# Low halves of g made by accumulating Pool transfers, row squares kept beside the x2 rows, and weight totals asked for three places later

## The chip, the core and the metric

The kernel runs on one core of one Trainium2 chip. The metric is the time of one execution in microseconds (us) on that core, taken as the median of several runs. The engines are named as in the profile: PE (TensorE), DVE (VectorE), ACT (ScalarE), POOL (GpSimd) and SP (SyncE, which here only issues transfers). Each engine works through its own instructions in order, and waits on semaphores for the others.

## The reference

Attention, a gated linear layer, and a routed layer with eight experts follow each other on 4608 tokens:

```python
scores = scale * np.matmul(q, k.transpose(0, 1, 3, 2))      # 8 x 8 heads, 576 x 576, block causal mask
...
attn = attn / (np.sum(attn, axis=-1, keepdims=True) + 1e-09)
return np.matmul(attn, v).astype(np.float32)
...
a = x @ w1                                                  # 512 -> 1024
b = x @ w2
h = a * b @ w3
return (h @ w_out).astype(np.float32)
...
logits = x @ w_gate                                         # 8 experts
order = np.argsort(-flat)
for idx in order:                                           # greedy: best pair first, 576 tokens per expert
    tok, e = (int(idx) // E, int(idx) % E)
    if assigned[tok] >= 0 or counts[e] >= cap:
        continue
    assigned[tok] = e
...
h = np.maximum(x[mask] @ w1[e], 0.0)                        # 512 -> 1024 -> 512
out[mask] = h @ w2[e]
```

## The kernel before

Products must be nearly exact, so every operand is split into a high half (rounded) and a low half (what the rounding lost), and each product is three matmuls: high by high, high by low, low by high.

The program has three stages. In the first (0 to about 838 us in the profile) attention runs head pair by head pair, and the products `a * b` of the gated layer (called g) are written to a DRAM tensor `gd`. `w3 @ w_out` has been multiplied out into one matrix of 1024 x 512, kept as `W34[0]` (high) and `W34[1]` (low), written by `load_w34`. At the end of this stage the logits of the router are formed.

In the second stage (about 838 to 1137 us) two things share PE. The **route** is a serial search: 7 phases of 9 levels, and in each level PE and DVE hand small results to each other. DVE makes `M` (L789), PE counts with it (L806), DVE makes `mk` (L821), PE sums it (L827), DVE makes `fl` (L830), PE sums it (L832), DVE makes `dl` (L834), and the next `M` follows. Between these small matmuls the **stream** is laid: `x2 = g @ W34`, 36 tiles of 128 tokens with 24 matmuls each (L965). `fill(n)` puts the next n stream matmuls into PE's program at that place, some 10 in each level. PE, Pool and ACT keep the order in which this stage is written (`manual_schedule`); the other engines' order, and all engines' order outside the stage, is set at build time by a scheduler that simulates the program.

A stream tile j needs its g split: `prep_g(j)` loads 128 tokens of g into `g32` (two buffers), ACT rounds them to the high half `gh` (L980), and DVE subtracts to get the low half `gl` (L982, two instructions). It is called two tiles ahead. When a tile is done, `x2_out` copies it from PSUM into `row` (ACT, L988) and SP stores it in the DRAM tensor `xr`. Weights of the first experts (`ew0`) are converted in the same stage, on ACT (L1038) and DVE (L1039).

In the third stage (from about 1137 us) the tokens of each expert are gathered from `xr` by Pool (`xg`, L1090, four buffers). ACT squares the row and adds it up (L1094), DVE turns the sum into a power of two (`pow2`), ACT scales to the high half (L1096), DVE makes the low half (L1097), and SP transposes (`xT`, L1098). PE then does `layer1` (L1121) and `layer2` (L1138) of each expert, while ACT and DVE prepare the next experts' weights in `expert_w`: load, eight squares (`red`, L1024), a matmul with ones that adds the squares over the partitions (`fin`, the **total**, L1029), and eight conversions (`conv`, L1038 and L1039). The list of these operations is interleaved with the list of matmul units in equal shares. The staging buffer of each weight (`esa`, `esb`) exists once, so a load waits until the last conversion before it is done.

Of the kernel before, what the change touches and what calls it, by code (L numbers as in the profile page):

```python
# [7 lines left out]
F32 = mybir.dt.float32  # L8
F32R = mybir.dt.float32r
F16 = mybir.dt.float16  # L10
BF16 = mybir.dt.bfloat16
I32 = mybir.dt.int32
AF = mybir.ActivationFunctionType
ALU = mybir.AluOpType
# [45 lines left out]
def moe_kernel(ctx, tc, q, k, v, moe_w1, moe_w2, moe_w3, moe_w_out, w_gate, ew1, ew2, out):  # L60
# [882 lines left out]

    xr = dram.tile([NTOK, DM], F32, name="xr")
    wl = pb.enter_context(tc.tile_pool(name="wl", bufs=1, reuse_waits="tile"))
# [4 lines left out]
    def load_w34():  # L950
        for f in range(0, 8, 2):
            t = gp.tile([P, 8, P], F32, name="g32").rearrange("p (f a) b -> p f (a b)", f=2)
            nc.sync.dma_start(t, w34d[f:f + 2].rearrange("f p d -> p f d"))
            nc.scalar.activation(W34[0][:, f:f + 2], t, AF.Copy)
            nc.gpsimd.tensor_tensor(out=W34[1][:, f:f + 2], in0=t, in1=W34[0][:, f:f + 2].bitcast(F32), op=ALU.subtract)

# [19 lines left out]
    def prep_g(j):  # L976
        g = gp.tile([P, 8, P], F32, name="g32")
        nc.sync.dma_start(g, gd[:, :, j * P:(j + 1) * P].rearrange("f p t -> p f t"))
        gh = [gp.tile([P, 8, P], F32R, name=f"g{z}") for z in "hl"]
        nc.scalar.activation(gh[0], g, AF.Copy)  # L980
        for f in range(0, 8, 4):
            nc.vector.tensor_tensor(out=gh[1][:, f:f + 4], in0=g[:, f:f + 4], in1=gh[0][:, f:f + 4].bitcast(F32),  # L982
                                    op=ALU.subtract)
        gt[j] = gh

    def x2_out(j, p):
        row = gp.tile([P, DM], F32, name="row", bufs=3)
        nc.scalar.activation(row, p, AF.Copy)  # L988
        nc.sync.dma_start(xr[j * P:(j + 1) * P], row)
# [93 lines left out]
    def gather(p):  # L1083
        def block(h):
            if h == 0:
                xT2[p] = ce.tile([P, 8, NG * P], F16, name="xT2")
                scs[p] = ce.tile([P, NG], F32, name="sc")
            xg = ce.tile([P, DM], F32, name="xg", bufs=4)
            c = p * NG + h
            nc.gpsimd.indirect_dma_start(out=xg, out_offset=None, in_=xr,  # L1090
                                         in_offset=bass.IndirectOffsetOnAxis(ap=idx[:, c:c + 1], axis=0))
            x16 = ce.tile([P, 2, DM], F16, name="x16", bufs=4)
            sq = ce.tile([P, 1], F32, name="sq2", bufs=4)
            nc.scalar.activation(x16[:, 1], xg, AF.Square, accum_out=sq)  # L1094
            s, i = pow2(ce, sq, "xsc", TBX, bufs=4)
            nc.scalar.activation(x16[:, 0], xg, AF.Copy, scale=s)  # L1096
            nc.vector.scalar_tensor_tensor(x16[:, 1], xg, s, x16[:, 0], op0=ALU.mult, op1=ALU.subtract)  # L1097
            nc.sync.dma_start_transpose(out=xT2[p][:, :, h * P:h * P + P], in_=x16.rearrange("p z d -> p (z d)"))  # L1098
            nc.vector.tensor_copy(scs[p][:, h:h + 1], i)

        return [lambda h=h: block(h) for h in range(NG)]
# [47 lines left out]
    def weights(e, part):  # L1149
        if (e, part) == (1, 1):  # L1150
            return owed_w
        return expert_w(e, part, 512, False) if 2 <= e < E else []

    for f in gather(0):
        f()
    for p_ in range(E // 2):
# [7 lines left out]
        interleave([lambda k_=k_: layer2(p_, k_) for k_ in range(4)],  # L1164
                   (expert_w(1, 1, 512, False) if e == 0 else []) + weights(e + 2, 0))
        interleave(list(layer1(e + 1, halves)), more[4:])
# [38 lines left out]
```

## Time and profile before

| | us |
|---|---|
| three runs | 1576.71, 1581.57, 1591.8 |
| median of the three | 1581.57 |
| the profiled execution's own time | 1578.55 |
| its span in the profile | 1576.7 |
| PE busy in the span | 1370.9 (87%) |
| DVE busy | 1031.7 (65%) |
| ACT busy | 909.0 (58%) |
| POOL busy | 93.4 (6%) |

The profile is of one execution. Its own time lies 1.9 us above its span, and 3.0 us below the median of the runs. PE is busiest, but the share is a mean over three stages with different limits, so the stages have to be read one by one.

### The profile page before, as it was taken

Reading aid. Unit: us, or ns where it says so; the run is one execution under the profiler, and the core shown is the slowest. Engines: PE = TensorE matmul, PEld = TensorE weight load, DVE = VectorE, ACT = ScalarE, POOL = GpSimd, SP = SyncE. Lnnn points to the kernel's source line nnn. Section 1 sums busy time; section 2 is a strip of 40 time slices with the busy share of each in tenths; the row PEclk is TensorE's granted clock in tenths of the full one; section 3 lists DMA queues with packets and bytes.
Section 4 is the critical chain, followed back from the end, with each engine's and each line's share of the span. In section 5 each row is a group of like instructions: output and inputs, shape, how many; then the busy total and the mean of one; then the engine's idle time right before and its main releaser. Section 6 shows DMA issues by size and latency. Waiting matters only on the chain. (4 is left out here: it accounts for less than half of the span.)

```text
span 1576.7 us, 32324 instructions
## 1 busy us (share of the span) xinstructions
PE 1370.9 (87%) x12622; PEld 932.3 (59%) x12622; DVE 1031.7 (65%) x3058; ACT 909.0 (58%) x2173; POOL 93.4 (6%) x101
## 2 busy tenths in 40 slices
PE   3457887999898999999999988899669979799897
PEld 2335665666666666666666665666466546466663
DVE  8889998868978887864215778878656543532510
ACT  8879886778868786654221223342167864855611
POOL 0000000000000000100200000000043300110001
PEclk9668999999999999999999999999789989899999
DMA  7767796887868785479945324333297653622200
GB/s 252 179 157 186 192 224 155 177 150 179 214 129 200 161 201 99 92 188 240 307 135 186 101 81 152 97 130 97 89 183 221 157 176 94 187 74 76 72 27 34
DMA packets 379657, 238.51 MB, mean 151 GB/s; under 512 B 261232, under 2 KB 344688, under 8 KB 378480
## 3 DMA queue, kind: packets, MB, share of 16 engines
q1 hardware_dynamic: 372064, 215.46, 53.8%
q0 software_dynamic: 5760, 18.88, 3.7%
q8 instruction: 99, 1.62, 0.4%
q10 hardware_dynamic: 1680, 2.11, 0.4%
q14 instruction: 54, 0.44, 0.1%
HBM read 132.60 MB, written 39.85 MB: 109 GB/s over the span
## 5 line engine op out<-in xcount | busy, mean ns | idle before, releaser
L325 PE MATMUL ab<-xT,w1h 128*128 128x288 f16 x1536 | 218.1, 291 | 14.1 <-ACT a_sb L330 10.7
L325 PE MATMUL ab<-xT,w2h 128*128 128x288 f16 x1536 | 219.5, 292 | 3.3 <-DVE g L335 2.1
L1121 PE MATMUL pe<-xT,ewa 128*128 128x288 f16 (+2 forms) x1728 | 200.7, 281 | 18.8 <-DMA xT<-x 13.6
L1121 PEld LDWEIGHTS <-ewa 128*128 128x128 f16 x1728 | 161.6, 102 | 56.9 <-issue 19.6
L1138 PE MATMUL pe<-ewb,h 128*128 128x512 f16 (+1 forms) x960 | 189.1, 379 | 0.0
L325 PEld LDWEIGHTS <-w1h 128*128 128x128 f16 x1536 | 145.3, 100 | 64.8 <-issue 24.1
L245 ACT ACTIVATE E<-S,nb,cc 128x128 f32<-128x128 f32 (+4 forms) x288 | 181.5, 639 | 2.8 <-DVE P L256 1.0
L325 PEld LDWEIGHTS <-w2h 128*128 128x128 f16 x1536 | 147.3, 100 | 57.0 <-issue 15.2
L256 DVE SCALAR_TENSOR_TENSOR P<-E,rr,P 128x512 f16<-128x512 f32 (+4 forms) x288 | 156.0, 573 | 10.7 <-ACT P L255 10.1
L980 ACT ACTIVATE gh<-g 128x1024 fp32r<-128x1024 f32 x36 | 38.1, 1059 | 204.2 <-issue 181.7
L1138 PEld LDWEIGHTS <-h 128*128 128x128 f16 (+1 forms) x960 | 85.3, 101 | 99.1 <-issue 2.6
L300 PE MATMUL PV<-PT,v 128*64 128x128 f16 (+1 forms) x2880 | 101.5, 223 | 48.0 <-DMA PT<-P 41.1
L1124 DVE SCALAR_TENSOR_TENSOR h<-pe,h 128x288 f16<-128x288 f32 (+2 forms) x144 | 58.8, 420 | 115.5 <-ACT h L1123 115.2
L300 PEld LDWEIGHTS <-v 128*64 128x64 f16 x2880 | 84.0, 117 | 73.3 <-issue 35.6
L965 PE MATMUL px<-W34l,gh 128*128 128x512 f32 x288 | 123.0, 427 | 0.0
L965 PE MATMUL px<-W34h,gh 128*128 128x512 f32 x288 | 122.4, 425 | 0.0
L335 DVE SCALAR_TENSOR_TENSOR g<-ab,vr,a_sb 128x288 f32<-128x288 f32 x124 | 63.5, 512 | 89.9 <-PE ab L325 74.1
L965 PE MATMUL px<-W34h,gl 128*128 128x512 f32 x288 | 122.2, 424 | 0.0
L255 ACT ACTIVATE P<-E,rr 128x128 f16<-128x128 f32 (+3 forms) x176 | 97.4, 604 | 23.9 <-DVE rr L249 15.6
L237 DVE TENSOR_REDUCE nb<-S 128x2 f32<-128x1024 f32 (+3 forms) x128 | 101.5, 813 | 3.6 <-PE S L228 3.5
L1123 ACT ACTIVATE h<-pe 128x288 f16<-128x288 f32 (+2 forms) x144 | 52.3, 378 | 85.4 <-PE pe L1121 85.4
L330 ACT ACTIVATE a_sb<-ab 128x288 f32<-128x288 f32 x128 | 52.2, 408 | 83.3 <-PE ab L325 79.0
(283 smaller groups left out, 2220.4 us busy)
## 6 DMA issues: line engine op xcount, KB each, us to landing
g<-gd SPq DMA_DIRECT2D x36, 512.0 KB, 3.8
gd<-g SPq DMA_DIRECT2D x62, 288.0 KB, 3.0
g<-gd SPq DMA_DIRECT2D x15, 1152.0 KB, 7.1
raw<-in_moe_w_dram SPq DMA_DIRECT2D x32, 512.0 KB, 4.5
esa<-in_moe_w_dram SPq DMA_DIRECT2D x8, 2048.0 KB, 8.7
esb<-in_moe_w_dram SPq DMA_DIRECT2D x8, 2048.0 KB, 9.5
v<-in_v_dram SPq DMA_DIRECT2D x8, 1280.0 KB, 6.2
xr<-row SPq DMA_DIRECT2D x36, 256.0 KB, 2.0
```

The lines of the kernel that those rows point to most:

```text
L237: nc.vector.tensor_reduce(nb[:, 0, k_:k_ + 2], ps[:, :, o:o + N], axis=AX.X, op=ALU.max)
L245: nc.scalar.activation(ef[:, a], pf_[:, a], AF.Exp, bias=nb[:, 1, x:x + 1], scale=c[:, 0:1], accum_out=sums[:, x:x + 1])
L255: nc.scalar.activation(hi, ef[:, at[x]], AF.Copy, scale=r[:, 1, x:x + 1])
L256: nc.vector.scalar_tensor_tensor(lo, ef[:, at[x]], r[:, 1, x:x + 1], hi, op0=ALU.mult, op1=ALU.subtract)
L300: nc.tensor.matmul(ps[hh * 64:hh * 64 + 64, c0:c0 + w], vt[:, zv, hh, j, :], s, start=z == 0 and j == 0, stop=z == 2 and j == nj - 1)
L325: nc.tensor.matmul(p[:, :288], w[:, zw, cc, :], x[:, zx, cc, c0:c0 + 288], start=first, stop=cc == 3 and zw == 1)
L335: nc.vector.scalar_tensor_tensor(g, ps["w2"][:, :288], iv[b][:, f:f + 1], a, op0=ALU.mult, op1=ALU.mult)
L965: nc.tensor.matmul(p, gh[a][:, f], W34[b][:, f], start=f == 0 and a + b == 0, stop=f == 7 and a == 1)
L1121: nc.tensor.matmul(p[:, :n], w1[:, a, cc, f * P:(f + 1) * P], t[:, 4 * b + cc, x], start=cc == 0 and a + b == 0, stop=cc == 3 and a == 1)
L1123: nc.scalar.activation(h[:, 0, f, x], p[:, :n], AF.Relu)
L1124: nc.vector.scalar_tensor_tensor(h[:, 1, f, x], p[:, :n], 0.0, h[:, 0, f, x], op0=ALU.max, op1=ALU.subtract)
L1138: nc.tensor.matmul(p[r0:r1], h[:, a, f, k_ * P + r0:k_ * P + r1], EW[e, "b"][0][:, b, f], start=f == 0 and a + b == 0, stop=f == 7 and a == 1)
```

## The change

Three edits are made at once.

1. **Low halves.** The low half of g is no longer a DVE subtraction. ACT writes the negated high half into the low half's tile (a copy with scale -1), and the high half as before; a Pool transfer with `accum_op=ALU.add` then adds g to the negated half in SBUF, which leaves g minus its high half. The four low halves of `W34`, which Pool subtracted, are made in the same way. `gh` and `gl` get three buffers in place of two.
2. **Row squares.** `x2_out` squares the finished tile straight from PSUM on ACT and adds it up into a 513th column of `row`. `xr` and `xg` get rows of 513 numbers, and the gather block no longer squares what it has gathered. `row` gets two buffers in place of three.
3. **Totals.** `expert_w` is asked for with `early=True` for the later experts, which puts three empty operations between the last square and the total.

```diff
-    xr = dram.tile([NTOK, DM], F32, name="xr")
+    xr = dram.tile([NTOK, DM + 1], F32, name="xr")
...
+            nc.scalar.activation(W34[1][:, f:f + 2], t, AF.Copy, scale=-1.0)
             nc.scalar.activation(W34[0][:, f:f + 2], t, AF.Copy)
-            nc.gpsimd.tensor_tensor(out=W34[1][:, f:f + 2], in0=t, in1=W34[0][:, f:f + 2].bitcast(F32), op=ALU.subtract)
+            nc.gpsimd.dma_start(W34[1][:, f:f + 2].bitcast(F32), t, accum_op=ALU.add)
...
-        gh = [gp.tile([P, 8, P], F32R, name=f"g{z}") for z in "hl"]
+        gh = [gp.tile([P, 8, P], F32R, name=f"g{z}", bufs=3) for z in "hl"]
+        nc.scalar.activation(gh[1], g, AF.Copy, scale=-1.0)
         nc.scalar.activation(gh[0], g, AF.Copy)
-        for f in range(0, 8, 4):
-            nc.vector.tensor_tensor(out=gh[1][:, f:f + 4], in0=g[:, f:f + 4], in1=gh[0][:, f:f + 4].bitcast(F32),
-                                    op=ALU.subtract)
+        nc.gpsimd.dma_start(gh[1].bitcast(F32), g, accum_op=ALU.add)
...
-        row = gp.tile([P, DM], F32, name="row", bufs=3)
-        nc.scalar.activation(row, p, AF.Copy)
+        row = gp.tile([P, DM + 1], F32, name="row", bufs=2)
+        jk = gp.tile([P, DM], F16, name="jk", bufs=1)
+        nc.scalar.activation(jk, p, AF.Square, accum_out=row[:, DM:])
+        nc.scalar.activation(row[:, :DM], p, AF.Copy)
...
-            sq = ce.tile([P, 1], F32, name="sq2", bufs=4)
-            nc.scalar.activation(x16[:, 1], xg, AF.Square, accum_out=sq)
-            s, i = pow2(ce, sq, "xsc", TBX, bufs=4)
-            nc.scalar.activation(x16[:, 0], xg, AF.Copy, scale=s)
+            s, i = pow2(ce, xg[:, DM:], "xsc", TBX, bufs=4)
+            nc.scalar.activation(x16[:, 0], xg[:, :DM], AF.Copy, scale=s)
...
-        return expert_w(e, part, 512, False) if 2 <= e < E else []
+        return expert_w(e, part, 512, True) if 2 <= e < E else []
...
-                   (expert_w(1, 1, 512, False) if e == 0 else []) + weights(e + 2, 0))
+                   (expert_w(1, 1, 512, True) if e == 0 else []) + weights(e + 2, 0))
```

Where the instructions stand now is shown at two places. The first is DVE in the third level of the route's second phase (near 891 us in the profile), from `mk` to `dl`. Before:

```order
L821 TENSOR_TENSOR mk<-p_13485,delta 128x32
L721 TENSOR_TENSOR T<-dp,iok 128x640
L982 TENSOR_TENSOR gl<-g_13366,gh 128x512 x2
L797 TENSOR_TENSOR R<-R,p_13495 128x8
L830 SCALAR_TENSOR_TENSOR fl<-R,p_13504 128x8
L834 TENSOR_REDUCE dl<-p_13513 128x1
```

Now:

```order
L821 TENSOR_TENSOR mk<-p_13507,delta 128x32
L721 TENSOR_TENSOR T<-dp,iok 128x640
L797 TENSOR_TENSOR R<-R,p_13517 128x8
L830 SCALAR_TENSOR_TENSOR fl<-R,p_13526 128x8
L834 TENSOR_REDUCE dl<-p_13535 128x1
```

The two subtractions ahead of `fl` are gone, and nothing has come in their place; so it is at all 36 tiles. The weight conversions (L1039) stay on DVE in the third, fifth and seventh phase.

The second place is ACT in the layer2 units of experts 0 and 1, between the squares of the b weights of expert 2 (`ewb,emb`) and their conversion (`ewb` x8); `x` with `sq` is the square of a gathered row, `x` alone its scaling. Before:

```order
L1024 ACTIVATE ewb,emb<-esb 128x512 x7
L1096 ACTIVATE x_18666<-xg,xsc 128x512
L1096 ACTIVATE x_18724<-xg,xsc 128x512
L1096 ACTIVATE x_18782<-xg,xsc 128x512
L1094 ACTIVATE x_18840,sq_18841<-xg 128x512
L1141 ACTIVATE y<-pe,s_16824 128x512
L1096 ACTIVATE x_18840<-xg,xsc 128x512
L1141 ACTIVATE y<-pe,s_16824 128x512
L1094 ACTIVATE x_18898,sq_18899<-xg 128x512
L1038 ACTIVATE ewb<-esb,epb 128x512 x8
```

Now (the lines are those of the changed kernel, two further down):

```order
L1026 ACTIVATE ewb,emb<-esb 128x512 x7
L1096 ACTIVATE x_18866<-xg,xsc 128x512
L1096 ACTIVATE x_18922<-xg,xsc 128x512
L1141 ACTIVATE y<-pe,s_16882 128x512
L1096 ACTIVATE x_19361<-xg,xsc 128x512
L1096 ACTIVATE x_19402<-xg,xsc 128x512
L1141 ACTIVATE y<-pe,s_16882 128x512
L1040 ACTIVATE ewb<-esb,epb 128x512 x8
```

The row square that stood last ahead of the conversion is gone, and the scalings of two later gathers have moved ahead of it.

On PE, every total of the expert stage stands behind the same number of matmuls as before: the totals of the b weights of experts 3, 5 and 7, for instance, still follow the 60th of the 192 `layer1` matmuls of experts 2, 4 and 6. With 21 operations dealt out over 8 units in place of 18, the total is the 13th in place of the 10th, and both fall behind the fifth unit. On PE's order in the route nothing changes either: 100 of the 864 stream matmuls stand ahead of the first routing matmul in both programs. Ahead of the route the first stream matmul now stands behind 2880 of the 3072 MoE matmuls (L325), where it stood behind 2796.

## Rows read from the trace of the kernel before

**Rows 1.** Windows by stage: busy us by engine, then granted clock, DMA share, GB/s.

```profile
760.00:838.00 78.00, 78.00 (x603) 51.78 (x602) 13.35 (x27) 17.04 (x34) 4.67 (x2) 1.00 0.59 191
838.00:1137.00 299.00, 264.74 (x1872) 184.64 (x1871) 230.86 (x931) 85.22 (x155) 0.00 (x0) 0.96 0.36 119
1137.00:1184.00 47.00, 28.17 (x391) 27.10 (x390) 24.39 (x110) 25.68 (x74) 19.45 (x19) 0.79 0.93 171
```

**Rows 2.** Waits of PE over the whole span: us in total, times, longest us.

```profile
PE p L806 <- DVE M L789: 13.4, 11, 3.0
PE p L827 <- DVE mk L821: 8.2, 12, 1.3
PE p L832 <- DVE fl L830: 8.0, 11, 2.4
PE p L936 <- DVE Bh L928: 3.4, 1, 3.4
PE pe L1029 <- ACT ewb L1024: 22.1, 3, 9.7
```

**Rows 3.** Timeline near 892 us: start, us, idle before and releaser.

```profile
891.03 1.29 DVE L982 TENSOR_TENSOR gl<-g,gh 128x512 fp32r<-128x512 f32 x2
892.72 0.17 PE L832 MATMUL p<-fl,q 128*128 128x8 f16 x1 [0.79 <-DVE fl L830]
```

**Rows 4.** Timeline of PE: waits behind weight conversions (L1039) on DVE.

```profile
927.79 0.17 PE L832 MATMUL p<-fl,q 128*128 128x8 f16 x1 [0.76 <-DVE fl L830]
1019.62 0.29 PE L806 MATMUL p<-M,T 128*128 128x32 f16 x5 [3.03 <-DVE M L789]
1109.53 0.17 PE L832 MATMUL p<-fl,q 128*128 128x8 f16 x1 [2.38 <-DVE fl L830]
```

**Rows 5.** Windows of 2 us after 927.79 us: the clock is third last.

```profile
928.00:930.00 2.00, 2.00 (x5) 1.29 (x5) 1.65 (x8) 0.00 (x0) 0.00 (x0) 0.50 0.46 137
932.00:934.00 2.00, 2.00 (x10) 1.38 (x9) 0.81 (x4) 0.00 (x0) 0.00 (x0) 0.50 0.00 0
```

**Rows 6.** Groups of instructions over the whole span: busy us, mean ns of one.

```profile
L980 ACT ACTIVATE gh<-g 128x1024 fp32r<-128x1024 f32 x36 | 38.1, 1059 | 204.2 <-issue 181.7 <-PE p L832 7.6 <-DMA g<-gd 6.6
L982 DVE TENSOR_TENSOR gl<-g,gh 128x512 fp32r<-128x512 f32 x72 | 46.4, 686 | 18.7 <-ACT gh L980 15.6 <-PE px L965 2.4 <-issue 0.2
L1094 ACT ACTIVATE x<-xg 128x512 f16<-128x512 f32 x36 | 22.4, 624 | 31.7 <-DMA xg<-xr,idx 21.2 <-DMA xT<-x 9.8 <-ACT x L1096 0.7
L1094 ACT ACTIVATION_READ_ACCUMULATOR x<-xg 128x1 f32 x36 | 6.8, 189 | 0.0
L1090 POOL DMA_INDIRECT xg<-xr,idx x36 | 39.4, 1095 | 434.8 <-DVE idx L941 371.0 <-DVE h L1124 21.3 <-DVE x L1097 15.2
```

**Rows 7.** DMA issues: count, KB each, median us from issue to landing.

```profile
g<-gd SPq DMA_DIRECT2D x36, 512.0 KB, 3.8
xr<-row SPq DMA_DIRECT2D x36, 256.0 KB, 2.0
xg<-xr,idx POOLq DMA_INDIRECT x36, 5.2
```

**Rows 8.** Timeline of ACT and PE ahead of expert 3's b total.

```profile
1247.40 0.63 ACT L1094 ACTIVATE x<-xg 128x512 f16<-128x512 f32 x1 [1.95 <-DMA xg<-xr,idx]
1248.03 1.32 ACT L1038 ACTIVATE ewb<-esb,epb 128x512 f16<-128x512 f32 x2
1266.35 0.63 ACT L1024 ACTIVATE ewb<-esb 128x512 f16<-128x512 f32 x1 [2.05 <-DMA esb<-in_moe_w_dram]
1272.00 0.60 PE L1029 MATMUL pe<-emb,ones 128*128 128x8 f32 x2 [9.75 <-ACT ewb L1024]
```

**Rows 9.** Timeline of PE: first matmul of the expert stage.

```profile
1151.01 1.22 PE L1121 MATMUL pe<-xT,ewa 128*128 128x128 f16 x10 [13.62 <-DMA xT<-x]
```

**Rows 10.** Timeline of Pool; then the group of MoE matmuls.

```profile
763.12 4.67 POOL L955 TENSOR_TENSOR W34l<-g,W34h 128x1024 fp32r<-128x1024 f32 x2 [3.75 <-ACT W34h L954]
L325 PE MATMUL ab<-xT,w1h 128*128 128x288 f16 x1536 | 218.1, 291 | 14.1 <-ACT a_sb L330 10.7
```

More of the change, by code (lines that the diff above doesn't have):

```diff
@@ L1087, in block @@
                 scs[p] = ce.tile([P, NG], F32, name="sc")
-            xg = ce.tile([P, DM], F32, name="xg", bufs=4)
+            xg = ce.tile([P, DM + 1], F32, name="xg", bufs=4)
             c = p * NG + h
@@ L1092, in block @@
             x16 = ce.tile([P, 2, DM], F16, name="x16", bufs=4)
-            sq = ce.tile([P, 1], F32, name="sq2", bufs=4)
-            nc.scalar.activation(x16[:, 1], xg, AF.Square, accum_out=sq)
-            s, i = pow2(ce, sq, "xsc", TBX, bufs=4)
-            nc.scalar.activation(x16[:, 0], xg, AF.Copy, scale=s)
-            nc.vector.scalar_tensor_tensor(x16[:, 1], xg, s, x16[:, 0], op0=ALU.mult, op1=ALU.subtract)
+            s, i = pow2(ce, xg[:, DM:], "xsc", TBX, bufs=4)
+            nc.scalar.activation(x16[:, 0], xg[:, :DM], AF.Copy, scale=s)
+            nc.vector.scalar_tensor_tensor(x16[:, 1], xg[:, :DM], s, x16[:, 0], op0=ALU.mult, op1=ALU.subtract)
             nc.sync.dma_start_transpose(out=xT2[p][:, :, h * P:h * P + P], in_=x16.rearrange("p z d -> p (z d)"))
```

## The prediction

> **What bounds the kernel now.** I read the windows by stage first, then PE's waits, then the timeline around single waits, because the three edits touch three stages with different limits.
>
> In the end of the first stage PE is busy for all of its 78 us [rows 1]: there every delay of a PE operand costs its full length, and nothing can be gained but work. In the route PE is busy for 264.7 of 299 us, DVE for 230.9, ACT for 85.2 only [rows 1]. So PE is nearly the bound, and what keeps it from being so is one list: it waits for `M` (13.4 us), `mk` (8.2) and `fl` (8.0), all of them DVE's links of the serial search, and once 3.4 us for `Bh` at the end [rows 2]. Near 892 us the reader sees such a wait whole: the two subtractions for `gl` take DVE from 891.03 for 1.29 us, `fl` can only follow them, and PE has stood still for 0.79 us when it gets it at 892.72 [rows 3]. DVE takes its instructions in order, so a subtraction that has nothing to do with the search sits in its chain. Not all waits are of this kind. Seven have weight conversions ahead of them on DVE: the first and the last, and the longest, are shown [rows 4], and the seven sum to 9.3 us.
>
> At the start of the expert stage PE is busy for 28.2 of 47 us at a mean granted clock of 0.79 [rows 1], and its first matmul waits 13.6 us for the first transposed gather [rows 9]. Later PE waits three times, 22.1 us in all, for the total of a b weight [rows 2].
>
> **The change part by part.**
>
> *Subtractions off DVE.* 72 instructions of 0.686 us [rows 6] leave DVE. Two of them stand at each tile, 1.29 us [rows 3], and no PE wait that has them ahead of it is longer than that but for the phase starts. So where they are the cause, the wait goes. That is 13.4 + 8.2 + 8.0 = 29.6 us [rows 2] less the 9.3 us behind conversions [rows 4]: **-20.3 us**. The other end is zero for those waits that the stream's own place in PE's program would set anyway; I take the whole, because the rows name DVE as releaser each time, and keep -12 as the weak end. What is late next is the conversions' 9.3 us and the 3.4 us for `Bh`, both of which stay.
>
> *Clock.* After the waits that end at 927.79 us [rows 4] the granted clock is 0.50, the lower level of 1.2 GHz, in the three windows from 928 to 934 us, of which the first and the last are shown [rows 5]. It is the second wait within two levels. Half of those 6 us is lost work: **-3.0 us** if the subtraction's share of that idleness goes. The two later low stretches follow conversions and stay. Ends: 0 and -3.7.
>
> *What replaces the subtraction.* ACT makes one more copy of 128x1024, 1.06 us [rows 6], and Pool issues one transfer per tile. The square of the finished tile adds 0.62 + 0.19 us [rows 6]. For some 33 tiles in the route that is 33 x 1.87 = 62 us more on ACT, which is busy 85 of 299 us: hidden, 147 of 299. If ACT's cover went, it would show as a late low half. The transfer is what no row shows. Call `a` the time from Pool's issue to landing of an accumulating transfer of 512 KB. A plain one of SP takes 3.8 us; Pool's gather of 256 KB takes 5.2; 256 KB more costs SP 3.8 - 2.0 = 1.8 us [rows 7]. That gives 3.8 us as the low end and 5.2 + 1.8 = 7.0 as an estimate for a Pool transfer of this size; as an accumulate must read its destination too, twice that, 14 us, is the high end. I take 7, since the gather is the nearest row.
>
> What may `a` be? A `g32` buffer is held through load, rounding and transfer, 3.8 + 1.06 + about half a us of hand-over + `a`, and there are two, so two tiles' time must cover it. A tile takes 299 / 33 = 9.1 us now and (299 - 23.3) / 33 = 8.35 after the gains: `a` up to 2 x 8.35 - 5.4 = 11.3 us costs nothing in the route, and every us above that costs 33 / 2 = 16.5 us. At 7 the route pays nothing.
>
> *Ahead of the route* the same transfers are tighter. Pool's subtraction took 4.67 / 2 = 2.3 us a piece [rows 10]; a transfer at 7 is 4.7 later. Two pieces of `W34` and then g's first tile follow each other through one buffer, so the first low half of g comes 3 x 4.7 = 14 us later, and with ACT's three extra copies up to 17. The program has moved its first use by 108 MoE matmuls of 218.1 / 1536 = 0.142 us [rows 10], 15.3 us. So the lateness is about -1 to +2, and PE has no idle time there to hide it [rows 1]: I charge **+2 us**, ends 0 and +4, and 3 us for each us of `a` above 7.5.
>
> *Row squares.* In the gather block a square (0.62 + 0.19 us) goes from in front of `pow2`, and the next row's square (0.62) from in front of the scaling: the first transposed block, for which PE waits at 1151.01 [rows 9], comes 1.4 us earlier. The next blocks go through a ring of four `xg` buffers, where a round gets shorter by the square alone: I add 1.1 us for all. **-2.5 us**, ends 0 and -5. The rows of 2052 bytes in place of 2048 are 0.2% more to move; what an odd row length costs no row shows, and I leave it inside the zero end. The store of the last tile gains 0.8 us of ACT ahead of it; it was done well ahead of `idx`, so nothing is charged.
>
> *Totals.* PE's program has the totals where they were, so the wait can't go by the edit itself; three empty operations cost nothing. What moves is ACT ahead of it. Before, the conversion of expert 2's b weight began at 1248.03, right behind a row square that had waited 1.95 us for its gather [rows 8]. The conversion frees `esb`, the load of expert 3's b follows, ACT then stood 2.05 us waiting for that load, began its squares at 1266.35, and PE got its total 9.75 us late at 1272.00 [rows 8]. Without the square, 1.95 + 0.63 = 2.6 us come off the whole chain. Expert 5 repeats the pattern; expert 7 has no gathers beside it. About 2 x 2.5 = **-5 us**, ends +2 (the two scalings now ahead of the conversion may wait for their own gathers) and -8; 22.1 [rows 2] would be all of it.
>
> **The sum.** -20.3 - 3.0 + 2.0 - 2.5 - 5.0 = -28.8 us. Against the profiled execution's own 1578.55 us that gives 1549.8, and as this execution lay 3.0 us below the median of its runs, 1552.8 for a median. With all weak ends: -12 + 0 + 4 + 0 + 2 = -6, so 1576; with all strong ends: -20.3 - 3.7 - 5 - 8 = -37, so 1545.
>
> **The rivals.**
>
> *The transfers are too slow* (slower). This takes the place of the subtraction as what PE waits for. From `a` = 11.3 the ring holds up the stream, and the entry ahead of the route pays from 7.5 on: at 12.3 the gain is used up (30.8 of gains without the 2, against 3 x 4.8 + 16.5 x 1.0 = 31), and at the high end of 14 the sum is -30.8 + 3 x 6.5 + 16.5 x 2.7 = +33, or 1615. For it speaks that nothing in the trace shows such a transfer, and that Pool's issue shares the stage with a DVE that is busy 77% of the time [rows 1]; against it that transfers of 256 and 512 KB land in 2.0 to 5.2 us [rows 7], and that DMA is busy for 0.36 of the route [rows 1]. The Trainium skill has a rule against this change: "SBUF — State Buffer", section "SBUF: two separate sides", says that Pool writes the descriptors of its transfers over a port pair that DVE locks in its two-port modes, so that such a transfer waits for DVE. If every busy moment of DVE were such a lock, Pool's issue of 1.1 us [rows 6] would stretch by 1 / 0.23 to 4.8 us, an estimate from that page and the busy share [rows 1]: `a` would be 10.7, under the ring's limit but 3 x 3.2 = 10 us dearer ahead of the route, and the time 1563; it counts with the forecast. No row of before shows a Pool transfer beside a busy DVE in the route. I give slow transfers 0.14.
>
> *The waits stay, under another name* (no change). Where the subtraction went, the next DVE work moves up, or PE's own stream order sets the pace: half of the 20.3 us goes, the clock stays low after conversions, and of the rest only the gather's 2.5 us comes: -10.2 + 2 - 2.5 = -10.7, or 1571. For it: DVE stays busy for 230.9 - 33 x 1.29 = 188 of some 276 us, and conversions remain in three phases. Against it: nothing has moved into the gaps on DVE. Chance 0.20.
>
> *The totals do move in effect* (faster still): if ACT's shift took all 22.1 us, the time would be 1536. The order on PE speaks against it; 0.04.
>
> **How the numbers follow.** Forecast 0.62, slow transfers 0.14, half the gain 0.20, more 0.04. Predicted: 1552.8, rounded to 1553. The forecast's own range is 1541 to 1566. For 8 in 10 the range goes up through the half gain to 1582 and down to 1540; it leaves out most of the slow case and the fastest. A measurement of this kernel can tell about 1%, 15.8 us, from no change: faster means below 1565.8, slower above 1597.4. Faster: the forecast, the fastest case and a little of the half gain, 0.67; slower: the upper part of the slow case, 0.11; same: 0.22.
>
> **What would show it.** In the route PE's waits for `M`, `mk` and `fl` should sum to about 9 us, all of them behind L1039 (now L1041) rows, with the stage some 23 us shorter. A PE wait whose releaser is a Pool transfer or ACT's copy, on the stream's line, would mean slow transfers; the landing time of that transfer against 7, 7.5 and 11.3 us says how much. PE idle ahead of 838 us shows the entry term. The b totals' waits should sum to about 17 us in place of 22.1, and the first `layer1` matmul should follow `idx` some 1.4 us sooner. The prediction is wrong if the low clock spreads, or if the search's chain turns out to be held by PE and not by DVE.

## The result and the profile after

The changed kernel takes **1556.55 us** (median of 4 runs, 1554.54 to 1560.58) against 1580.49 us for the kernel before on the same chip: a ratio of 0.985, 95% interval 0.982 to 0.989. The forecast was 1553. The profiled execution took 1554.94 us at a span of 1553.2 us, 23.5 us under the span of before.

Line numbers have moved by one to three: the stream's matmul is L966, the copies for the two halves of `g` L981 and L982, the accumulating transfer L983, the total of a weight L1031, the conversions L1040 (ACT) and L1041 (DVE). First the route, from its first count matmul (L806) to the start of the last stream matmul, as one window for each kernel; columns as in [rows 1]. Of before:

```profile
850.50:1130.90 280.40, 252.42 (x1779) 175.41 (x1779) 219.29 (x903) 81.13 (x149) 0.00 (x0) 0.96 0.35 114
```

and after:

```profile
855.80:1109.90 254.10, 243.39 (x1779) 170.08 (x1779) 185.45 (x842) 128.22 (x242) 25.86 (x30) 0.98 0.76 196
```

The route is 26.3 us shorter. PE runs the same 1779 matmuls in both. It stands still for 10.7 us in place of 28.0, and is busy for 9.0 us less, most of it because the granted clock is higher. DVE has lost 33.8 us of work, ACT has gained 47.1. PE's waits over the whole span, to be held against [rows 2]:

```profile
PE pe L1031 <- ACT ewb L1026: 22.1, 3, 12.9
PE p L936 <- DVE Bh L928: 3.4, 1, 3.4
PE p L806 <- DVE M L789: 3.3, 5, 0.8
PE lgp L388 <- ACT lgT L380: 2.9, 1, 2.9
PE p L827 <- DVE mk L821: 2.8, 2, 1.5
PE p L832 <- DVE fl L830: 2.6, 4, 1.1
PE px L966 <- DMA gl<-g: 1.3, 1, 1.3
```

The three waits of the search have gone from 29.6 to 8.7 us. The total of a b weight stands where it was, at 22.1 us. Two waits are new: 2.9 us for `lgT` and 1.3 us for a low half of `g`. On the timeline of PE the new waits and the ones that matter below are these:

```profile
747.92 0.25 PE L300 MATMUL PV<-PT,v 128*64 128x128 f16 x2 [2.49 <-DMA PT<-P]
773.89 0.22 PE L388 MATMUL lgp<-i,lgx 128*64 128x8 f32 x1 [2.90 <-ACT lgT L380]
855.76 0.38 PE L806 MATMUL p<-M,T 128*128 128x32 f16 x9
1008.06 0.24 PE L827 MATMUL p<-mk,selk 128*128 128x8 f16 x4 [1.50 <-DVE mk L821]
1128.66 1.55 PE L1121 MATMUL pe<-xT,ewa 128*128 128x128 f16 x13 [12.26 <-DMA xT<-x]
1250.10 0.60 PE L1031 MATMUL pe<-emb,ones 128*128 128x8 f32 x2 [12.90 <-ACT ewb L1026]
1352.11 0.60 PE L1031 MATMUL pe<-emb,ones 128*128 128x8 f32 x2 [4.70 <-ACT ewb L1026]
1454.12 0.60 PE L1031 MATMUL pe<-emb,ones 128*128 128x8 f32 x2 [4.52 <-ACT ewb L1026]
```

The DMA issues, to be held against [rows 7]:

```profile
g<-gd SPq DMA_DIRECT2D x36, 512.0 KB, 5.1
gl<-g POOLq DMA_DIRECT2D x36, 512.0 KB, 6.1
xr<-row SPq DMA_DIRECT2D x36, 256.5 KB, 5.7
```

The accumulating transfer lands 6.1 us after its issue, and the plain transfers beside it have become slower: `g` from 3.8 to 5.1, the finished rows from 2.0 to 5.7 us. Most of the latter is the traffic: in the kernels below with transfers and rows of 512 values it is 4.3 to 4.5 us, with rows of 513 it is 4.8 to 5.9.

For a ledger the last long wait for `PT` serves as a mark; in the kernel before it and the first count matmul were

```profile
744.98 0.25 PE L300 MATMUL PV<-PT,v 128*64 128x128 f16 x2 [2.53 <-DMA PT<-P]
850.54 0.38 PE L806 MATMUL p<-M,T 128*128 128x32 f16 x9 [2.88 <-DVE M L789]
```

| stretch (marks on PE) | before | after | difference |
|---|---|---|---|
| start to that wait for `PT` | 745.0 | 747.9 | +2.9 |
| to the first count matmul | 105.6 | 107.8 | +2.3 |
| route, to the last stream matmul | 280.4 | 254.2 | -26.2 |
| to the first `layer1` matmul | 20.1 | 18.7 | -1.4 |
| to the first `layer2` matmul | 32.8 | 30.1 | -2.8 |
| to the last `layer2` matmul | 383.8 | 385.0 | +1.2 |
| to the end | 9.1 | 9.5 | +0.4 |

The first line is not the change's: ahead of that mark all kernels here give the engines the same work (e4 one memset of Pool more), and their executions put it anywhere from 742.9 to 752.4 us.

### The profile page after: what moved, and what is told of

The parts are those of the page before. It is cut to its first block, busy times and chain, and to the rows that moved or that the text cites. A ratio compares the mean times of both kernels' runs of the same rounds, so it can differ in the third digit from the quotient of the medians.

```text
span 1553.2 us, 32385 instructions
## 1 busy us (share of the span) xinstructions
PE 1370.7 (88%) x12622; PEld 933.2 (60%) x12622; DVE 987.8 (64%) x2986; ACT 947.5 (61%) x2213; POOL 118.6 (8%) x137
## 5 line engine op out<-in xcount | busy, mean ns | idle before, releaser
L325 PE MATMUL ab<-xT,w1h 128*128 128x288 f16 x1536 | 222.5, 295 | 12.7 <-ACT a_sb L330 9.3
L325 PE MATMUL ab<-xT,w2h 128*128 128x288 f16 x1536 | 221.0, 294 | 3.8 <-DVE g L335 2.3
L325 PEld LDWEIGHTS <-w1h 128*128 128x128 f16 x1536 | 147.4, 101 | 64.6 <-issue 21.7
L325 PEld LDWEIGHTS <-w2h 128*128 128x128 f16 x1536 | 148.5, 100 | 57.0 <-issue 14.0
L966 PE MATMUL px<-W34h,gl 128*128 128x512 f32 x288 | 120.2, 418 | 1.3 <-DMA gl<-g 1.3
L966 PE MATMUL px<-W34h,gh 128*128 128x512 f32 x288 | 120.9, 420 | 0.0
L966 PE MATMUL px<-W34l,gh 128*128 128x512 f32 x288 | 120.4, 418 | 0.0
L330 ACT ACTIVATE a_sb<-ab 128x288 f32<-128x288 f32 x128 | 52.1, 407 | 71.6 <-PE ab L325 71.5
L224 PE MATMUL S<-qkT 64*128 64x512 f16 (+3 forms) x768 | 78.6, 317 | 12.6 <-ACT E L245 12.6
```

The costliest lines, as they stand in the source:

```text
L224: nc.tensor.matmul(ps[:, hh, o:o + N], tq[r, a, m * P:m * P + P], tk[r, b, :N], start=a + b == 0, stop=False)
L325: nc.tensor.matmul(p[:, :288], w[:, zw, cc, :], x[:, zx, cc, c0:c0 + 288], start=first, stop=cc == 3 and zw == 1)
L966: nc.tensor.matmul(p, gh[a][:, f], W34[b][:, f], start=f == 0 and a + b == 0, stop=f == 7 and a == 1)
```

## The experiments

All times are medians; a ratio is to the kernel before in the same session, with its 95% interval. "Entry" is the second stretch of the ledger, "route" the third.

**e1: the transfers of `g` alone.** Everything else as before.

```
-        gh = [gp.tile([P, 8, P], F32R, name=f"g{z}") for z in "hl"]
+        gh = [gp.tile([P, 8, P], F32R, name=f"g{z}", bufs=3) for z in "hl"]
+        nc.scalar.activation(gh[1], g, AF.Copy, scale=-1.0)
         nc.scalar.activation(gh[0], g, AF.Copy)
-        for f in range(0, 8, 4):
-            nc.vector.tensor_tensor(out=gh[1][:, f:f + 4], ..., op=ALU.subtract)
+        nc.gpsimd.dma_start(gh[1].bitcast(F32), g, accum_op=ALU.add)
...
-        row = gp.tile([P, DM], F32, name="row", bufs=3)
+        row = gp.tile([P, DM], F32, name="row", bufs=2)
```

> Low halves of g by transfers, everything else as before (W34 by Pool's subtraction, squares in the gather, no empty operations). Theory A (the gain is DVE relieved in the route): the search's waits of PE for M, mk and fl fall from 29.6 to about 9 us, the stretch from the first count matmul of the route to the last stream matmul falls from 280.8 to about 255 us as in the changed kernel (254.5), the entry ahead of the route costs nothing because W34 keeps Pool's subtraction: about 1580.5 - 26 = 1554 us, as fast as the whole change without its row squares and totals. Rival B (the row squares and the totals carry half of the gain): no more than 12 us faster than before, 1568 us.

Measured: 1555.43 us, 0.986 (0.981 to 0.991). Route 252.1 us, waits for `M`, `mk` and `fl` 9.3 us. This one edit gives the whole gain: theory A, but for the entry, 107.1 us in place of 105.6, where nothing was expected.

**e2: the low half of W34 by Pool's subtraction again.**

```
-            nc.scalar.activation(W34[1][:, f:f + 2], t, AF.Copy, scale=-1.0)
             nc.scalar.activation(W34[0][:, f:f + 2], t, AF.Copy)
-            nc.gpsimd.dma_start(W34[1][:, f:f + 2].bitcast(F32), t, accum_op=ALU.add)
+            nc.gpsimd.tensor_tensor(out=W34[1][:, f:f + 2], in0=t, in1=W34[0]..., op=ALU.subtract)
```

> The changed kernel with the low half of W34 made by Pool's subtraction again; its route and expert stage are untouched. Theory A (the transfers of W34 hold the two load buffers, ACT's next copy waits 4.26 us for the load, the logits' copy stands behind it, PE waits 2.9 us and the clock falls): the wait of 2.9 us near 774 us and the low clock behind it go, the route starts 5 us sooner: 1556.5 - 5 = 1551.5 us. Rival B (g's own first transfers are what comes late ahead of the route): the route starts within 1 us of where it does in the changed kernel, 1556 us.

Measured: 1557.43 us, 0.987 (0.982 to 0.993). The wait for `lgT` is gone, and in its place stand, in the waits of PE from 740 to 860 us, two on the stream's line:

```profile
PE px L965 <- DMA gl<-g: 2.5, 1, 2.5
PE px L965 <- ACT gh L981: 0.6, 1, 0.6
```

The entry is 109.9 us. Theory A fell: it saw one of two latenesses, and the second, of `g`'s own first tile, was right behind it. Rival B had the place right.

**e3: the row squares in the gather again.** The hunks of `xr`, `x2_out` and `gather` in the diff are undone.

> The changed kernel with the row squares computed in the gather again (rows of 512 values, as before). Theory A (without the square on ACT, DVE's scale waits itself for the gather, ahead of the weight conversion, so expert 3's total comes late, which eats what the entry gains): the first layer1 matmul follows the index 1.4 us later and expert 0's layer1 takes 2.7 us longer, expert 3's total waits 7 to 10 us in place of 12.9; in all within 2 us of the changed kernel, 1555 to 1559 us. Rival B (the row squares are worth their forecast 2.5 us or more and the longer wait has another cause): expert 3's total still waits 12 us or more and the time is 1560 us or above.

Measured: 1556.27 us, 0.984 (0.979 to 0.989). The totals of experts 3, 5 and 7 wait 8.35, 8.32 and 4.52 us (after: 12.90, 4.70, 4.52; before: 9.75, 7.93, 4.38). The first `layer1` matmul follows the last stream matmul 19.3 us later in place of 18.7, and expert 0's `layer1` takes 30.0 us, as after, not 2.7 more. So theory A holds for the time and for expert 3's total, and is wrong on `layer1`. What made expert 3's total late shows on DVE of the changed kernel:

```profile
1226.75 0.15 DVE L78 TENSOR_SCALAR xsc<-xg 128x1 int32<-128x1 int32 x1 [1.93 <-DMA xg<-xr,idx]
1227.07 2.07 DVE L1041 SCALAR_TENSOR_TENSOR ewb<-esb,epb,ewb 128x512 f16<-128x512 f32 x3
1229.90 2.73 DVE L1041 SCALAR_TENSOR_TENSOR ewb<-esb,epb,ewb 128x512 f16<-128x512 f32 x4
```

and on SP and ACT:

```profile
1232.66 0.37 SPq L1019 DMA_DIRECT2D esb<-in_moe_w_dram  x1
```
```profile
1244.46 0.63 ACT L1026 ACTIVATE ewb<-esb 128x512 f16<-128x512 f32 x1 [4.41 <-DMA esb<-in_moe_w_dram]
```

The scale no longer waits for a square of ACT but for the gather itself, 1.93 us, and DVE's low halves of expert 2's b weight stand behind it. They end at 1232.6, SP issues the load of expert 3's b at 1232.66, and ACT gets it at 1244.46. The wait has changed engines. ACT's half of the conversion was no earlier either; it now waited for a small result of DVE:

```profile
1224.31 3.17 ACT L1040 ACTIVATE ewb<-esb,epb 128x512 f16<-128x512 f32 x5 [1.64 <-DVE epb L80]
```

Counted from the first `layer2` matmul, ACT's half begins at 65.6 us (before: 64.2), DVE's at 68.4 (64.9), and the load goes out at 73.9 (70.4; in e3 71.5). The load itself takes as long as before, 11.8 us against 12.1.

**e4: zeros ahead of each transfer.** A transfer of 128 KB of zeros is added to the low half first, so the load buffer is held longer and the result is the same.

```
+        nc.gpsimd.dma_start(gh[1][:, :2].bitcast(F32), zz, accum_op=ALU.add)
         nc.gpsimd.dma_start(gh[1].bitcast(F32), g, accum_op=ALU.add)
```

> The changed kernel with a second accumulating transfer ahead of each one of g: zeros, 128 KB, added to a quarter of the low half, so that the result is the same and the load buffer is held longer, by an estimated 3 to 5 us (a becomes 9 to 11 us). Forecast's ring limit (a up to 11.3 us costs nothing in the route): the route stays within 3 us, only the entry ahead of it is longer by 3 us per us, if g's transfers lie on it: 1557 to 1570 us. Theory B (with the loads of g at 5.1 us and two copies of 2.1 us, two tiles of 7.8 us leave only 15.6 - 7.7 = 7.9 us): the route is longer by 16.5 us for every us above 7.9, some 20 to 50 us, 1577 to 1607 us, with PE's waits on the stream's line.

Measured: 1567.17 us, 0.993 (0.990 to 0.996). The zeros land in 2.9 us, `g`'s transfer in 6.0, the load in 4.1:

```profile
gl<-zz POOLq DMA_DIRECT2D x36, 128.0 KB, 2.9
```

In the route PE now waits for the low half:

```profile
PE px L968 <- DMA gl<-g: 11.7, 9, 2.6
```

The route is 275.4 us, 21.3 more than after; the entry, 107.9, is the same. Theory B for the route, at its lower end; the time itself is 10 us under theory B's and within the range given to the forecast's limit. A buffer is held for load, two copies and transfer: 5.1 + 2.1 + 6.1 = 13.3 us after, 4.1 + 2.1 + 2.9 + 6.0 = 15.1 here. At 31.8 tiles in the route (764 stream matmuls of 24 a tile) each us that counts costs 15.9; 21.3 us are 1.3 us that count out of 1.8. So the changed kernel's ring has about half a us to spare. That is an estimate and a low one, since only 11.7 of the 21.3 us are waits for the low half and most of the rest goes with a granted clock of 0.94 in place of 0.98; by these waits alone 0.7 us count, and 1.1 are to spare.

**e5: the b totals later.** For experts 2, 4 and 6 the next expert's b weight and the four gathers change places among the `layer1` units.

```
-        interleave(units[:len(units) // 2], weights(e + 1, 1))
-        interleave(units[len(units) // 2:], more[:4])
+        w = weights(e + 1, 1)
+        interleave(units[:len(units) // 2], w if e == 0 else more[:4])
+        interleave(units[len(units) // 2:], more[:4] if e == 0 else w)
```

> The changed kernel with the b weights of experts 3, 5 and 7 (load, squares, total, conversion) interleaved with the second half of the layer1 units ahead of them in place of the first, and the four gathers with the first; so the total stands 8 units of about 1.47 us, 11.8 us, later on PE. Theory A (the total waits for a load, not for ACT's order, and three empty operations cannot move it; only a later place on PE can): the three waits sum to under 5 us in place of 22.1, and the time is 12 to 18 us shorter, 1538 to 1545 us. Rival B (the load chain only passes its lateness on, to the next weights or to layer2): the waits turn up under another name and the time is 1552 us or above.

Measured: 1536.49 us, 0.972 (0.969 to 0.976). From the first to the last `layer2` matmul 360.9 us in place of 385.0. No total waits there; all that PE waits for in that stretch is

```profile
PE pe L1121 <- DVE h L1124: 5.6, 2, 4.4
```

The stretch shows what the totals had cost besides their 22.1 us; after, and then here:

```profile
1158.70:1543.70 385.00, 362.88 (x2333) 223.58 (x2330) 150.50 (x383) 201.75 (x466) 54.19 (x52) 0.96 0.38 112
```
```profile
1165.90:1526.80 360.90, 355.35 (x2332) 220.08 (x2330) 150.34 (x386) 201.03 (x468) 54.30 (x52) 1.00 0.41 120
```

PE is busy for 7.5 us less with the same work, at a granted clock of 1.00 in place of 0.96. Theory A.

**e6: the route's weight conversions on Pool.** Their low halves were the DVE work that the search still waited for.

```
-                nc.vector.scalar_tensor_tensor(lo, w, d["sc"], hi, op0=ALU.mult, op1=ALU.subtract)
+                if late is None:
+                    nc.vector.scalar_tensor_tensor(lo, w, d["sc"], hi, op0=ALU.mult, op1=ALU.subtract)
+                else:
+                    nc.gpsimd.tensor_scalar(w, w, d["sc"], None, op0=ALU.mult)
+                    nc.gpsimd.tensor_tensor(out=lo, in0=w, in1=hi, op=ALU.subtract)
```

> The changed kernel with the low halves of the first three weight conversions, those that lie in the route, made by Pool (a scaling in place and a subtraction) in place of DVE. Theory A (what is left of the search's waits, 8.7 us, stands behind these conversions on DVE, and the low clock of the route behind the waits): the waits for M, mk and fl fall under 3 us, the route is 7 to 12 us shorter than 254.1 us, 1545 to 1550 us in all. Rival B (Pool's subtractions, 1.2 us for 512 values by the 2.3 us that 1024 took before, stand ahead of the transfers of g, whose ring has little room): waits for the low half of g on the stream's line appear and the time is 1557 us or above.

Measured: 1564.78 us, 0.990 (0.986 to 0.993). The waits for `fl` are gone and `M` waits 2.0 us, but the route is 262.6 us: the stream waits 5.2 us for low halves, and `mk` waits once for 5.59. DVE, Pool and PE near that wait:

```profile
1027.58 5.68 DVE L854 TENSOR_TENSOR A<-A,ab 128x36 f16<-128x36 f16 x1
```
```profile
1028.06 4.70 POOL L1045 TENSOR_TENSOR ewb<-esb,ewb 128x512 f16<-128x512 f32 x4
```
```profile
1033.41 0.25 PE L827 MATMUL p<-mk,selk 128*128 128x8 f16 x4 [5.59 <-DVE mk L821]
```

An addition that takes 0.18 us elsewhere took 5.68 while Pool ran four subtractions. Beside Pool's scalings it was not held:

```profile
1020.52 0.18 DVE L854 TENSOR_TENSOR A<-A,ab 128x36 f16<-128x36 f16 x1
```
```profile
1019.00 4.69 POOL L1044 TENSOR_SCALAR esb<-esb,epb 128x512 f32<-128x512 f32 x3
```

Rival B, and with one more mechanism than it named.

**e7: the entry as before.** W34 as in e2, and for the first two tiles of `g` the subtraction on DVE.

```
-        nc.scalar.activation(gh[1], g, AF.Copy, scale=-1.0)
+        if j >= 2:
+            nc.scalar.activation(gh[1], g, AF.Copy, scale=-1.0)
         nc.scalar.activation(gh[0], g, AF.Copy)
-        nc.gpsimd.dma_start(gh[1].bitcast(F32), g, accum_op=ALU.add)
+        if j >= 2:
+            nc.gpsimd.dma_start(gh[1].bitcast(F32), g, accum_op=ALU.add)
+        else:
+            ...
```

> The changed kernel with the low halves of W34 made by Pool's subtraction and those of the first two tiles of g by DVE's, as before; all other tiles by transfers. Theory A (what the changed kernel pays ahead of the route is the lateness of the first low halves, of W34 or of g's first tile alike): no PE wait for the logits' copy or for the low half near 770 to 785 us, and the stretch from the last long wait for the transposed probabilities to the first count matmul is 103 to 105 us in place of 107.8; 1552 to 1554 us. Rival B (DVE's or ACT's load there has another cause): 107 us or more, 1556 us.

Measured: 1561.42 us, 0.985 (0.981 to 0.990). The entry is 104.0 us and neither new wait is there: theory A for the place. In the time it does not show, since this execution's route took 258.6 us, the way from there to the first `layer2` matmul 3.7 us more than after and the rest of the expert stage 2.1 more; the run as a whole can't be told from the changed kernel.

**e8: e5, e6 and e7 together.**

> The three edits of the runs beside this one together. If the gains add: 1556.5 - 15 - 9 - 3 = 1529 us. If one of them only moves a wait, 1540 us or above.

Measured: 1533.49 us, 0.969 (0.965 to 0.972). The gains don't quite add up to 1529, and e6's part, alone a loss, is among them. DVE is held once here too, this time on an `M`, for which PE then waits 6.1 us:

```profile
1019.94 5.80 DVE L789 TENSOR_TENSOR M<-oh,eq 128x288 f16<-128x288 f16 x1
```
```profile
1020.42 4.71 POOL L1050 TENSOR_TENSOR ewb<-esb,ewb 128x512 f16<-128x512 f32 x4
```

**e9: e5 and e7 together, conversions on DVE.**

> The changed kernel with the totals later and the entry as before (W34 by Pool's subtraction, the first two tiles of g by DVE's, all others by transfers); the route's weight conversions stay on DVE. Theory A (Pool's subtractions beside DVE are what made the run with conversions on Pool slow: there DVE's addition for A took 5.68 us in place of 0.18): the route is 254 to 259 us again without a wait of over 2 us for mk or M, 104 us from the last long wait for the transposed probabilities to the first count matmul; 1536.5 - 4 = 1532 us. Rival B (the gain of the entry is taken back in the route, since the stream then starts with its tiles nearer to their use): 1537 us or above.

Measured: 1530.85 us (6 runs, 1522.7 to 1538.07), 0.969 (0.966 to 0.973). Entry 103.8, route 255.5, no wait for `mk` over 1.3 or for `M` over 2.1 us. Theory A, if `M`'s 2.1 is taken for its 2. Against e8, which differs by the conversions on Pool alone, it is 2.6 us less, within the intervals (the route 3.6 less): the 8 us that e6 lost to the changed kernel are not seen again there. Against e5 it is 5.6 us less, which the intervals don't tell apart either.

**e10: e9 without the row squares** (undone as in e3).

> The run beside this one, but with the row squares in the gather as before and rows of 512 values. Theory A (the row squares are worth next to nothing: the first transposed block comes 0.5 to 1.4 us sooner, and what ACT saves later DVE waits for the gather): within 3 us of the run beside it. Rival B (with the totals out of the way the row squares' shorter gather shows: 0.8 us for each of 36 blocks on ACT): 4 us or more slower than the run beside it.

Measured: **1521.67 us** (6 runs, 1511.98 to 1526.84), 0.963 (0.960 to 0.967), the best version here, 3.7% under the kernel before. Both theories missed the sign: without the row squares it is 9.2 us faster by the medians, with intervals that just touch. The profiles don't say why. Their spans are 6.1 us apart, and 5.65 of those lie ahead of the mark, where the two do the same work; e9 first, then e10:

```profile
750.19 0.25 PE L300 MATMUL PV<-PT,v 128*64 128x128 f16 x2 [2.53 <-DMA PT<-P]
```
```profile
744.54 0.25 PE L300 MATMUL PV<-PT,v 128*64 128x128 f16 x2 [2.44 <-DMA PT<-P]
```

Behind the mark e10 is 4.0 us shorter in the route, 4.4 longer up to the first `layer2` matmul, 1.5 shorter behind that, and 0.7 longer in the entry.

**e11: e5 with three load buffers for two.** To make room the finished row has one buffer, and its square is first written into that row.

```
-        g = gp.tile([P, 8, P], F32, name="g32")
+        g = gp.tile([P, 8, P], F32, name="g32", bufs=3)
...
-        row = gp.tile([P, DM + 1], F32, name="row", bufs=2)
+        row = gp.tile([P, DM + 1], F32, name="row", bufs=1)
```

> The changed kernel with the totals later and three load buffers for W34 and g in place of two (one buffer for the finished row, whose square is written into the row first). Theory A (the ring of two is what holds up the third load of W34 and, through ACT, the logits' copy, and what gives the one wait for a low half in the route): the PE wait of 2.9 us for the logits' copy and the low clock behind it are gone or below 1 us, no wait for the low half in the route; 3 to 6 us less than with the totals later alone, 1531 to 1534 us. Rival B (the transfer's own landing time is what comes late, buffers or not): waits of 2 us or more on PE between 765 and 790 us stay; 1536 us or above.

Measured: 1549.71 us, 0.980 (0.977 to 0.983), 13 us worse than e5. The wait for `lgT` is gone, but the fourth load of W34 now does what the third did: ACT, then PE,

```profile
778.67 1.06 ACT L954 ACTIVATE W34l<-g 128x1024 fp32r<-128x1024 f32 x1 [6.19 <-DMA g<-w34d]
```
```profile
781.02 3.04 PE L325 MATMUL ab<-xT,w1h 128*128 128x288 f16 x12 [4.76 <-ACT a_sb L330]
```

A third buffer only passes the lateness on: rival B for the wait that stays. In the route ACT stands 69.4 us for the store of the one row buffer, so its 265.1 us say nothing of the ring.

**e12: e10 with the storing half of the row squares.** Rows of 513 with the square in the last value, which the gather does not use.

> The kernel of the run with the totals later, the entry as before and the squares in the gather (1521.7 us; 1530.9 with the row squares), to which the storing half of the row squares is added again: rows of 513 values with the square in the last, which the gather then brings along and does not use, but squares the row itself as before. Theory A (what costs 9 us is the gather's half: DVE's scale waits for the gather itself, ahead of DVE's weight conversions): about 1522 us, within 3. Theory B (the storing half costs: a square more on ACT for each tile of the route, and rows of 2052 bytes): 1528 us or above, and the route longer than 251.5 us by 3 or more.

Measured: 1525.12 us, 0.967 (0.963 to 0.970), halfway between e10 and e9, whose intervals it touches both. Route 255.1 us, as theory B asks, but two executions of one route program differ as much (254.2 us after and 258.3 in e5); the time, 3.1 us above 1522, lies just outside theory A's 3. Which half of the row squares costs, and how much, stays open.

## Why the prediction was right, and where it was not

The total was right within 4 us, and so was the main mechanism. Of the terms, the clock, the entry and the totals were mis-sized, with errors of both signs, and that these nearly cancel is luck: e1, without the row squares and totals that were forecast at -7.5 us together, is as fast as the whole change.

*Subtractions off DVE* (-20.3): the search's waits fell by 20.9 us. The 8.7 us that are left were forecast as 9.3 behind conversions, and that is where they are, all eleven waits of them: around the wait at 1009.93 DVE has

```profile
1008.40 1.41 DVE L1041 SCALAR_TENSOR_TENSOR ewb<-esb,epb,ewb 128x512 f16<-128x512 f32 x2
1009.72 0.15 DVE L830 SCALAR_TENSOR_TENSOR fl<-R,p 128x8 f16<-128x8 f32 x1
```

e1 shows that this edit alone carries the result. The rival "under another name" is out: the stretch is shorter by all of it. The one new wait on the stream's line is 1.3 us.

*Clock* (-3.0): mis-sized. PE's busy time in the route fell by 9.0 us. The granted clock was at the lower level of 1.2 GHz for some 24 us of the route before (from 927.7, 1019.9 and 1108.7 us) and for 10 after (from 1009.7 and 1091.6). Half of the difference, 7 us, is what that can have cost; the other 2 stay open. The low stretch at 928 us went, as forecast; but the two behind later conversions, which "follow conversions and stay", became shorter too. One of them before, and then after:

```profile
1019.90:1026.70 6.80, 6.62 (x34) 4.67 (x34) 4.51 (x19) 0.00 (x0) 0.00 (x0) 0.50 0.55 178
```
```profile
1009.70:1013.10 3.40, 2.93 (x7) 1.82 (x6) 3.40 (x9) 1.71 (x3) 0.00 (x0) 0.50 0.29 82
```

The longest wait behind a conversion is now 1.5 us, against 3.03 and 2.38 in [rows 4], though their sum is nearly the same. A sum of waits doesn't give the clock's share. How much of it is the change's is not settled by one execution: the route of e5 is the same program on every engine, and there the low stretches sum to 20 us and the route is 4.1 us longer:

```profile
857.40:1115.70 258.30, 246.96 (x1779) 172.36 (x1779) 185.61 (x844) 128.49 (x242) 25.99 (x30) 0.96 0.77 194
```

*Transfer time* (7 us): 6.1 in the route, close, for the reason given. The ring's limit of 11.3 was wrong. The working held a buffer for one copy in place of two and for a load of 3.8 us, which the new traffic (DMA share 0.35 to 0.76) made 5.1; by the estimate under e4 the limit lies half a us to one us above where the kernel stands. The rival of slow transfers was nearer than its 0.14. The Trainium skill's rule ("SBUF — State Buffer", section "SBUF: two separate sides"), by which Pool's descriptors wait for DVE in its two-port modes, was weighed as 1563 us; here all 36 issues lie between 860 and 900 ns:

```profile
L983 POOL DMA_DIRECT2D gl<-g x36: 860/860/900, 792.8 to 1085.7; - x36
```

with DVE busy for 185 of 254 us. The trace shows no such lengthening of the issue.

*Ahead of the route* (+2): mis-sized. The entry is 2.3 us longer although the 2.88 us wait for the first `M` is no longer in it, so the charge is 5.2; against the five kernels with the old entry (e7 to e10 and e12, 103.6 to 104.4 us) it is 3.4 to 4.3. The forecast's own rate, 3 us for each us of `a` above 7.5, comes near that: ahead of the route `a` was not the route's 6.1 but

```profile
W34l<-g POOLq DMA_DIRECT2D x4, 512.0 KB, 8.2
```

which makes the +2 a +4.1. That one `a` was taken for both places is what the term got wrong, and the place of the wait. The forecast had the first low half late by -1 to +2 us and looked for the wait on the stream's line. It came elsewhere. SP could not issue the third load of W34 until a transfer had freed the buffer, ACT waited for it with its next copy, and `lgT` stood behind that copy on ACT. SP's waits from 755 to 775 us, then ACT:

```profile
SPq L953 <- DMA W34l<-g: 10.6, 2, 9.0
```

```profile
771.54 1.06 ACT L954 ACTIVATE W34l<-g 128x1024 fp32r<-128x1024 f32 x1 [4.26 <-DMA g<-w34d]
773.45 0.39 ACT L380 ACTIVATE lgT<-lgp 128x288 f32<-128x288 f32 x1
```

so PE stood for 2.90 us, and then ran at the lower level of 1.2 GHz, as in this window of 2 us:

```profile
776.00:778.00 2.00, 2.00 (x10) 1.29 (x9) 0.18 (x1) 1.21 (x2) 0.00 (x0) 0.50 1.10 329
```

e2, e7 and e11 show both lateness and cure: only with W34 and the first two tiles of `g` off the transfers is the entry shorter than before.

*Row squares* (-2.5): the first transposed block comes 1.4 us sooner, as forecast, though e3 puts only 0.6 us of it down to the row squares, and expert 0's `layer1` scatters between 27.9 and 34.8 us over all runs. At its own place the term is borne out on the mean: from the last stream matmul to the first `layer2` matmul the seven kernels that gather ready squares take 49.4 us and the five that square in the gather 52.6 (e6 and e8, with conversions on Pool, left out). In the time it does not show: once the totals are out of the way the version without row squares is the faster one by the medians, and no run shows what pays for it.

*Totals* (-5): wrong; 22.1 us before and after. The forecast took 2.6 us off ACT and the whole chain behind it. ACT's conversion came no earlier, as it waited for DVE (the rows under e3). And the same edit made DVE's scale wait for the gather ahead of the conversion's other half, so the load went out 3.5 us later, expert 3 lost 3.15 us and expert 5 gained 3.23. With the totals at their place, the sum was 20.6 to 23.8 us in all eight kernels; the weak end, +2, was the one to take. That empty operations do nothing was right, and e5 shows what does: a later place on PE.

Against -28.8 the profiled execution shows -23.5: PE's busy time in the route fell by 6.0 us more than the clock's -3.0 and the way from the route to the first `layer2` matmul 1.6 more; the entry took 3.2 more, the rest of the expert stage 6.2 more than with the totals' -5, the stream's new wait 1.3, and 2.9 lie ahead of the mark. Smaller pieces are left out.

## What to carry to other kernels

Taking work that nobody waits for out of the queue of the engine that holds a serial chain is worth the waits behind it and some of the clock behind these waits; look for the price where the substitute is first used and its buffers are not yet turning, and count every step for which a ring's buffer is held, at the durations under the new traffic. When an operation leaves one engine, ask which engine now meets the wait that it had been absorbing. The wait for a load was not shortened here by thinning the queues ahead of it, but went when the waiting instruction got a later place: e5's three lines were worth nearly as much as the whole change.

## What the hardware showed unexpectedly

DVE stood through several instructions of Pool in a row. In e6 its 128x36 addition took 5.68 us in place of 0.18, and in e8 an `M` took 5.80; both ended only behind four Pool subtractions back to back, 4.70 us in all. The Trainium skill ("SBUF — State Buffer", section "SBUF: two separate sides") calls the shared port pair an exclusive lock that is held for the whole instruction; the trace agrees that DVE is blocked outright, but here it did not get the pair between one Pool instruction and the next. Not every Pool instruction blocks it: beside Pool's scalings, which read and write SBUF as well, the same addition took 0.18 us.

An accumulating transfer of 512 KB from SBUF to SBUF took 6.1 us to land, little more than a plain load's 5.1 us beside it, not twice as much; one of 128 KB took 2.9. Ahead of the route, at a DMA share of 0.88 from 760 to 838 us, four such transfers took 8.2. Transfers of other queues became slower beside them: the store of a finished row went from 2.0 us to between 4.3 and 4.5 with rows of 512 values.
